# Stacking 64-token halves as even and odd lanes on the way into a 2-D Fourier filter

## The chip, the cores and the metric

One core of a Trainium2 chip runs the whole kernel. The metric is the device time of one execution in microseconds (us); the smaller, the better.

## The reference, cut to what matters

```python
x  = A_x                                  # (1, 2048, 512), bf16
xn = layernorm(x, axis=-1)                # no scale, no bias, eps 1e-5

# A: a global filter in the frequency domain, over tokens and channels
X = rfft2(xn)                             # (2048, 257), complex
y = irfft2(X * (A_w_r + 1j * A_w_i), s=(2048, 512)).astype(bf16)

# B: a gated MLP, 512 -> 1792 -> 512
g, u = xn @ B_w_gate, xn @ B_w_up
return x + y + (gelu_tanh(g) * u) @ B_w_down
```

## The kernel before, in words

**Two bodies of work on five engines.** TensorE (PE) computes the MLP, and matmuls with small cosine and sine matrices for the Fourier part. VectorE (DVE) computes LayerNorm's statistics, the products `gelu(g) * u`, and all sums and differences of the Fourier part. ScalarE (ACT) moves matmul results out of PSUM (L662 applies gelu, L663 copies, L576, L787, L865 and L929 copy results of the Fourier part). GpSimd takes inverse roots, SyncE (SP) issues nearly all DMAs, one after the other, in one queue.

**The order of the work** is written by a planner that runs while the program is built (`_Sched`). Each operation is declared with its engine, an assumed cost and a key. `run` goes through a simulated time: it takes next the operation that could start first, among those of the same engine within 0.05 us the one with the smallest ready time plus key. A PE operation whose inputs come from elsewhere counts as ready 1.0 us late (`MARGIN`, L245). Each engine then runs its list strictly in that order and waits on semaphores. `pool` gives names to small sets of buffers: 3 PSUM banks for `gu` (the MLP's first products), 2 pairs of banks for `sp` (everything of the Fourier part, and the last block's `down`), 1 bank for `dn`, 4 SBUF buffers each for `gg` and `uu`, 28 for `hT`.

**The MLP** is the filler of PE's list. `gated` (L648) makes 8 matmuls for one of 14 column groups of one block of 512 tokens, two evictions on ACT (L662 into `gg`, L663 into `uu`) and one product on DVE (L664 into `hT`, key 1.5). `down` (L692) makes 14 matmuls for 128 tokens, an eviction (L710) and an addition to `x` on DVE (L711); for the last block, DVE adds straight from PSUM (L713).

**The Fourier part** is one long chain, cut into these steps:
1. `stats`, `norm` and `turn` (L503 to L539): LayerNorm of 16 row blocks of 128 tokens, and transposes into `xnT`, 4 row blocks at a time.
2. `fold(b)` (L545), for each group b of 4 row blocks: DVE folds the channels (4 operations), then pairs row blocks, the sum and the difference of one and the mirrored other (L558, L559), into `z`. PE multiplies with the channel transform (L570), 8 matmuls for each of 2 row blocks, and ACT evicts to `Y` (L576).
3. The slot transform (L742 to L764): DVE transforms over 8 slots, for even and odd token parts side by side, from `Y` through `s_`, `v_`, `ab` to `H`, 14 operations.
4. The token matmuls (L767 to L787): for each of 8 groups v of frequencies, the cosine and sine matrices of `tokf` times `H`. Groups 0 and 1 take 2 matmuls, the other six 4: cosine times one part plus sine times the other, for the real and the imaginary result. ACT evicts to `X` (L787).
5. The filter (L794 to L843) on DVE, the way back through tokens (L859, L860) and a 16-slot transform on DVE (L868 to L906), the way back through channels (L924), and the addition to `x` (L937).

`x` is loaded and stored in 16 row blocks; row block s holds tokens of block `(s - 1) % 16` (`blk`, L458). The first four are loaded by one DMA each (L466 to L470), before the weights in SP's queue.

Of the kernel before, what the change touches and what calls it, by code (L numbers as in the profile page):

```python
# [12 lines left out]
S = 2048  # L13
D = 512
FF = 1792
P = 128
# [20 lines left out]
def _constants():  # L37
# [13 lines left out]
    cof[:, 0, 0] *= 0.5  # L51
    tf = np.stack([cof, si2, -si2], 1)
    ci, sv = co[:64].transpose(2, 1, 0), si2[:64].transpose(2, 1, 0)
# [32 lines left out]
class _V:  # L86


    def __init__(self, ap, buf, idx, cell):
        self.ap, self.buf, self.idx, self.cell = ap, buf, idx, cell  # L90

    def __getitem__(self, sl):
        if not isinstance(sl, tuple):
            sl = (sl,)
        return _V(self.ap[sl], self.buf, self.idx[sl[1:]], self.cell)

    def rs(self, shape):
        nd = self.idx.ndim
        ap = self.ap
        names = "abcdef"  # L100
        if nd > 1:
            ap = ap.rearrange("p %s -> p (%s)" % (" ".join(names[:nd]), " ".join(names[:nd])))
        if len(shape) > 1:
            nn = names[:len(shape)]
            ap = ap.rearrange("p (%s) -> p %s" % (" ".join(nn), " ".join(nn)), **dict(zip(nn[1:], shape[1:])))
        return _V(ap, self.buf, self.idx.reshape(shape), self.cell)

    def tr(self, perm):
        names = "abcdef"[:len(perm)]
        ap = self.ap.rearrange("p %s -> p %s" % (" ".join(names), " ".join(names[i] for i in perm)))  # L110
        return _V(ap, self.buf, self.idx.transpose(perm), self.cell)

    def cells(self):
        return [(self.buf, int(c)) for c in np.unique(self.idx // self.cell)]

# [217 lines left out]
def bass_parallel_sum__spectral_gfnet__glu_gated_geglu__prompt_kernel(  # L333
# [14 lines left out]

    xb = A_x[0].rearrange("(a q) d -> q a d", q=P)
    ob = out[0].rearrange("(a q) d -> q a d", q=P)  # L350
    wgv = B_w_gate.rearrange("(dc p) f -> p dc f", p=P)
# [6 lines left out]
    with ExitStack() as es:  # L358
# [22 lines left out]
        small = sb("smallc", [11, P])  # L381
        tf = sb("tokf", [3, 8, P])
        ti = sb("toki", [8, 3, P])
# [73 lines left out]

        def blk(s):  # L458
            return (s - 1) % 16

        def wload(q, dst, src, lo, hi, **kw):
# [79 lines left out]

        Y = R1(0, [8, 2, D])
        H = R3(0, [8, 2, D])
        X = R1(0, [8, 2, D])
        def fold(b):  # L545
            par = b % 2
            a = RB(2048 * par, [4, 2, P])
            f = RB(4096 + 2048 * par, [4, 4, P])
            z = R3(2048 * par, [2, 2, 512])
            xt = xnT[:, b]  # L550
# [4 lines left out]
            tt(f[:, :, 2:4], xt[:, :, 0:2], xt[:, :, 2:4], SUB, 1024, kk)  # L555
            fv = f.rs([2, 2, 4, P])
            zv = z.rs([2, 2, 4, P])
            tt(zv[:, :, 0], fv[:, :, 1], fv[:, :, 0, :, ::-1], ADD, 1024, kk)  # L558
            tt(zv[:, :, 1], fv[:, :, 1], fv[:, :, 0, :, ::-1], SUB, 1024, kk)  # L559
            for j in range(2):  # L560
                t = _T("sp")

                def f_c(e, z=z, j=j, t=t):
                    ins = None
                    for o in range(2):
                        bank = spb(t, o).rearrange("p (s r i) -> p s r i", s=2, r=4)
                        for cc in range(4):
                            to = bank[:, :, 2 * cc] if cc < 2 else bank[:, :, 1::2]
                            mat = Tf.ap[:, cc] if cc < 2 else Tf.ap[:, 2 * cc - 2:2 * cc]
                            ins = e.matmul(to, z.ap[:, j, o, cc * P:(cc + 1) * P], mat, start=(cc == 0), stop=(cc == 3))  # L570
                    return ins

                op("pe", 4 * 0.057 + 4 * 0.11, f_c, reads=(z[:, j], Tf), tiles=(t,), key=kk, lag=0.1)
                jp = 2 * b + j
                yv = Y[:, jp].rs([4, 64, 4])
                op("act", c_act(1024), lambda e, yv=yv, t=t: e.activation(yv.ap, spair(t).rearrange("p (s r i) -> p s i r", s=4, r=4), ACT.Copy),  # L576
                   writes=(yv,), tiles=(t,), key=-0.5)
# [30 lines left out]
        load("sp", wd, wdv, NFC * 131072, key=next(k))  # L608
        load("sp", tf, c_tf.ap().rearrange("p (t v m) -> p t v m", t=3, v=8), 786432, key=next(k))
        load("sp", ti, c_ti.ap().rearrange("p (v t q) -> p v t q", v=8, t=3), 786432, key=next(k))  # L610
# [104 lines left out]
        def store(s0, n, lo=0, w=512):  # L715
            for s in range(s0, s0 + n):
                v = xs(s)[:, lo:lo + w]
                o = op("sp", 0.41, lambda e, s=s, v=v: e.dma_start(ob[:, blk(s), lo:lo + w], v.ap), reads=(v,), dma=256 * w, key=0.0)
                sch.finals.append(o)

# [20 lines left out]

        s_ = RB(0, [4, 1024])  # L742
        v_ = RB(4096, [4, 1024])
        ab = RB(8192, [2, 1024])
        Yf = R1(0, [8, 1024])
        Hf = R3(0, [8, 1024])

        def scale(v, n):
            op("dve", c_ts(n), lambda e: e.tensor_scalar(v.ap, v.ap, float(np.sqrt(0.5)), None, MUL), reads=(v,), writes=(v,))

        tt(s_[:, 0:2], Yf[:, 0:2], Yf[:, 4:6], ADD, 2048)
        tt(v_[:, 0:2], Yf[:, 0:2], Yf[:, 4:6], SUB, 2048)
        tt(s_[:, 2:4], Yf[:, 2:4], Yf[:, 6:8], ADD, 2048)
        tt(v_[:, 2:4], Yf[:, 2:4], Yf[:, 6:8], SUB, 2048)
        tt(ab[:, 0], v_[:, 1], v_[:, 3], SUB, 1024)
        tt(ab[:, 1], v_[:, 1], v_[:, 3], ADD, 1024)
        scale(ab, 2048)
        tt(Hf[:, 4:6], s_[:, 0:2], s_[:, 2:4], SUB, 2048)
        tt(s_[:, 0:2], s_[:, 0:2], s_[:, 2:4], ADD, 2048)
        tt(Hf[:, 0], s_[:, 0], s_[:, 1], ADD, 1024)  # L760
        tt(Hf[:, 1], s_[:, 0], s_[:, 1], SUB, 1024)
        tt(Hf[:, 2:4], v_[:, 0::2], ab, ADD, 2048)
        tt(Hf[:, 6], v_[:, 0], ab[:, 0], SUB, 1024)
        tt(Hf[:, 7], ab[:, 1], v_[:, 2], SUB, 1024)  # L764

        CO, SI, NS = 0, 1, 2
        for v in range(8):  # L767
            c = v // 2
            t = _T("sp")
            if c == 0:  # L770
                seq = ((0, ((CO, H[:, v, 0]),)), (1, ((SI, H[:, v, 1]),)))
                rd = H[:, v]
            else:
                hr, hi = H[:, 2 * c], H[:, 2 * c + 1]
                seq = ((0, ((CO, hr[:, 0]), (NS, hi[:, 1]))), (1, ((CO, hi[:, 0]), (SI, hr[:, 1]))))
                rd = H[:, 2 * c:2 * c + 2]

            def f_t(e, v=v, t=t, seq=seq):
                ins = None
                for r, terms in seq:  # L780
                    for i, (mt, h) in enumerate(terms):
                        ins = e.matmul(spb(t, r), tf.ap[:, mt, v, :], h.ap, start=(i == 0), stop=(i == len(terms) - 1))  # L782
# [91 lines left out]

        def ts(o, a, f, n):
            op("dve", c_ts(n), lambda e: e.tensor_scalar(o.ap, a.ap, float(f), None, MUL), reads=(a,), writes=(o,))

        tt(al[:, 8], U[:, 0], U[:, 1], ADD, 512)
# [31 lines left out]
        for jq in range(4):  # L910
            js = slice(2 * jq, 2 * jq + 2)
            for lo, hi in ((0, 1), (1, 4)) if jq == 0 else ((4 * jq, 4 * jq + 4),):
                a = Yi[:, (lo - 1) % 16:(lo - 1) % 16 + hi - lo]
                tt(zi[:, lo:hi, :, 0:64], a[:, :, 0], a[:, :, 1], ADD, 256 * (hi - lo))
            a = Yi[:, 4 * jq:4 * jq + 4]
            tt(zi[:, 4 * jq:4 * jq + 4, :, 127:63:-1], a[:, :, 0], a[:, :, 1], SUB, 1024)
            for jp in (2 * jq, 2 * jq + 1):
                t = _T("sp")

                def f_b(e, jp=jp, t=t):  # L920
                    ins = None
                    for o in range(2):
                        for cc in range(4):
                            ins = e.matmul(spb(t, o, cc * P, P), zi.ap[:, 2 * jp + o, cc, :], Ti.ap[:, cc, :], start=(cc == 0), stop=(cc == 3))  # L924
                    return ins

                op("pe", 8 * 0.0565, f_b, reads=(zi[:, 2 * jp:2 * jp + 2], Ti), tiles=(t,), lag=0.1)
                rv = R[:, jp].rs([1024])
# [47 lines left out]
```

## Time and profile before

| what | value |
|---|---|
| median of 3 runs | 178.88 us (178.66 to 179.46) |
| the profiled execution, its own time | 178.78 us |
| its span in the profile | 177.0 us |
| PE busy | 172.4 us (97%), 1052 matmuls |
| DVE busy | 137.8 us (78%), 270 instructions |
| ACT busy | 106.4 us (60%), 172 instructions |
| DMA moved | 14.97 MB |

The span runs from the first instruction to the last; 1.78 us of the execution lie around it. Matmuls are pipelined, so one matmul's duration is longer than the time between the starts of two. The chain of work that ended last gives the time that each piece holds up its successor, and the timeline gives start and duration of each instruction.

### The profile page before, as it was taken

Reading aid. Unit: us, or ns where it says so; the run is one execution under the profiler, and the core shown is the slowest. Engines: PE = TensorE matmul, PEld = TensorE weight load, DVE = VectorE, ACT = ScalarE, POOL = GpSimd, SP = SyncE. Lnnn points to the kernel's source line nnn. Section 1 sums busy time; section 2 is a strip of 40 time slices with the busy share of each in tenths; the row PEclk is TensorE's granted clock in tenths of the full one; section 3 lists DMA queues with packets and bytes.
Section 4 is the critical chain, followed back from the end, with each engine's and each line's share of the span. In section 5 each row is a group of like instructions: output and inputs, shape, how many; then the busy total and the mean of one; then the engine's idle time right before and its main releaser. Section 6 shows DMA issues by size and latency. Waiting matters only on the chain.

```text
span 177.0 us, 2757 instructions
## 1 busy us (share of the span) xinstructions
PE 172.4 (97%) x1052; PEld 90.8 (51%) x1052; DVE 137.8 (78%) x270; ACT 106.4 (60%) x172; POOL 10.1 (6%) x19
## 2 busy tenths in 40 slices
PE   7889999999999999999999999999999999999994
PEld 2678665456554444444544644445664444444443
DVE  3869899999969939999999799999599812121931
ACT  3478775658685798363894966363995636362000
POOL 2120420300000230000000000000000000000000
DMA  5999997222363710000000000000004200000311
GB/s 167 335 351 356 349 371 266 61 65 47 66 151 87 176 38 4 0 0 0 0 6 0 0 0 0 0 4 0 0 19 132 91 0 0 0 4 0 119 59 61
DMA packets 17773, 14.97 MB, mean 85 GB/s; under 512 B 1119, under 2 KB 17376, under 8 KB 17760
## 3 DMA queue, kind: packets, MB, share of 16 engines
q1 hardware_dynamic: 16560, 13.94, 26.3%
q10 hardware_dynamic: 1200, 0.85, 1.6%
q8 instruction: 8, 0.13, 0.3%
q14 instruction: 5, 0.04, 0.1%
HBM read 12.70 MB, written 3.15 MB: 90 GB/s over the span
## 4 chain that ended last, share of the span: by engine, by line
PE 93%; DMA 5%; SPq 1%; issue 0%; DVE 0%
PE ps_gu L657 53%; PE ps_dn L702 20%; PE ps_sp L702 7%; PE ps_sp L782 3%; DMA wu<-in_B_w_up_dram 3%; PE ps_sp L570 3%; PE ps_sp L924 2%; PE ps_sp L534 2%; DMA x_sb<-in_A_x_dram 1%; PE ps_sp L859 1%; PE ps_sp L860 1%; SPq L446 1%; DVE x_sb L713 0%
## 5 line engine op out<-in xcount | busy, mean ns | idle before, releaser
L657 PE MATMUL ps_gu<-xnT,wu 128*128 128x512 bf16 (+1 forms) x236 | 56.7, 363 | 0.6 <-DMA wu<-in_B_w_up_dram 0.6
L657 PE MATMUL ps_gu<-xnT,wg 128*128 128x512 bf16 (+1 forms) x236 | 56.7, 363 | 0.0
L663 ACT ACTIVATE uu<-ps_gu 128x512 bf16<-128x512 f32 (+1 forms) x59 | 33.9, 574 | 13.2 <-PE ps_gu L657 12.9
L662 ACT ACTIVATE gg<-ps_gu 128x512 bf16<-128x512 f32 (+1 forms) x59 | 34.0, 576 | 12.2 <-PE ps_gu L657 11.6
L702 PE MATMUL ps_dn<-wd,hT 128*128 128x512 bf16 x168 | 38.5, 379 | 0.0
L657 PEld LDWEIGHTS ps_gu<-xnT,wu 128*128 128x128 bf16 x236 | 22.7, 98 | 22.9 <-ACT uu L688 0.8
L657 PEld LDWEIGHTS ps_gu<-xnT,wg 128*128 128x128 bf16 x236 | 22.6, 98 | 21.5 <-DVE xnT L539 0.3
L664 DVE TENSOR_TENSOR hT<-gg,uu 128x512 bf16<-128x512 bf16 (+1 forms) x59 | 22.7, 394 | 11.6 <-ACT uu L663 11.5
L702 PEld LDWEIGHTS ps_dn<-wd,hT 128*128 128x128 bf16 x168 | 16.4, 98 | 19.4
L450 DVE TENSOR_TENSOR specB<-specB 128x1024 bf16<-128x1024 bf16 (+2 forms) x37 | 23.5, 669 | 2.1 <-ACT specB L929 2.0
L710 ACT ACTIVATE db<-ps_dn 128x512 bf16<-128x512 f32 x12 | 7.2, 597 | 23.4 <-PE ps_dn L702 23.4
L504 DVE BATCH_NORM_STATS2 bst<-x_sb 128x6 f32<-128x512 bf16 x16 | 10.9, 685 | 3.7 <-DMA x_sb<-in_A_x_dram 3.5
L450 DVE TENSOR_TENSOR specB<-specA 128x2048 bf16<-128x2048 bf16 x8 | 9.4, 1220 | 4.0 <-ACT specA L787 2.1
L702 PE MATMUL ps_sp<-wd,hT 128*128 128x512 bf16 (+2 forms) x70 | 12.3, 336 | 0.0
L711 DVE TENSOR_TENSOR x_sb<-db,x_sb 128x512 bf16<-128x512 bf16 x12 | 5.0, 418 | 7.8 <-ACT db L710 7.8
L450 DVE TENSOR_TENSOR specC<-specB 128x1024 bf16<-128x1024 bf16 (+1 forms) x14 | 10.0, 759 | 0.0
L702 PEld LDWEIGHTS ps_sp<-wd,hT 128*128 128x128 bf16 x70 | 6.4, 98 | 6.1 <-DVE x_sb L713 0.2
L450 DVE TENSOR_TENSOR specB<-specB,filt 128x2048 bf16<-128x2048 bf16 x8 | 9.4, 1215 | 0.0
L787 ACT ACTIVATE specA<-ps_sp 128x1024 bf16<-128x1024 f32 x8 | 7.9, 1027 | 2.0 <-PE ps_sp L782 1.9
L929 ACT ACTIVATE specB<-ps_sp 128x1024 bf16<-128x1024 f32 x8 | 8.5, 1090 | 0.0
L576 ACT ACTIVATE specA<-ps_sp 128x1024 bf16<-128x1024 f32 x8 | 7.8, 1021 | 0.3
L865 ACT ACTIVATE specC<-ps_sp 128x1024 bf16<-128x1024 f32 x8 | 7.8, 1042 | 0.0
(63 smaller groups left out, 141.2 us busy)
## 6 DMA issues: line engine op xcount, KB each, us to landing
out_dram<-x_sb SPq DMA_DIRECT2D x15, 128.0 KB, 1.8
wd<-in_B_w_down_dram SPq DMA_DIRECT2D x1, 1792.0 KB, 13.3
x_sb<-in_A_x_dram SPq DMA_DIRECT2D x3, 512.0 KB, 8.4
wg<-in_B_w_gate_dram SPq DMA_DIRECT2D x2, 512.0 KB, 8.4
wu<-in_B_w_up_dram SPq DMA_DIRECT2D x2, 512.0 KB, 8.7
filt<-w_mirror SPq DMA_DIRECT2D x6, 128.5 KB, 2.3
tokf<-c_tf SPq DMA_DIRECT2D x1, 768.0 KB, 13.7
toki<-c_ti SPq DMA_DIRECT2D x1, 768.0 KB, 9.7
```

The costliest lines, as they stand in the source:

```text
L450: return op("dve", c_tt(n), lambda e: e.tensor_tensor(o.ap, a.ap, b.ap, f), reads=(a, b), writes=(o,), key=key, **kw)
L504: op("dve", 0.61, lambda e: e.bn_stats(bst[:, s].ap, xs(s).ap), reads=(xs(s),), writes=(bst[:, s],), key=key, due=due, after=after)
L576: op("act", c_act(1024), lambda e, yv=yv, t=t: e.activation(yv.ap, spair(t).rearrange("p (s r i) -> p s i r", s=4, r=4), ACT.Copy), writes ...
L657: ins = e.matmul(gub(t, n), w.ap[:, dc, fc * P:(fc + 1) * P], xnT.ap[:, b, sl, dc, :], start=(dc == 0), stop=(dc == 3))
L662: op("act", c_act(n), lambda e: e.activation(gg.ap[:, gs.slot, 0:n], gub(g, n), ACT.Gelu_apprx_tanh), tiles=(g, gs), key=0.0)
L663: op("act", c_act(n), lambda e: e.activation(uu.ap[:, us.slot, 0:n], gub(u, n), ACT.Copy), tiles=(u, us), key=0.0)
L664: op("dve", c_tt(n), lambda e: e.tensor_tensor(hT.ap[:, h.slot, lo:lo + n], gg.ap[:, gs.slot, 0:n], uu.ap[:, us.slot, 0:n], MUL), tiles=(g ...
L702: ins = e.matmul(bank(), hT.ap[:, hs[(b, fc)].slot, sl * P:(sl + 1) * P], wd.ap[:, fc, lo:lo + n], start=(fc == 0), stop=(fc == NFC - 1))
L710: op("act", c_act(n), lambda e: e.activation(db.ap[:, d.slot, 0:n], bank(), ACT.Copy), tiles=(t, d), key=0.0)
L787: op("act", c_act(1024), lambda e, xv=xv, t=t: e.activation(xv.ap, spair(t), ACT.Copy), writes=(xv,), tiles=(t,), key=-0.5)
L865: op("act", c_act(1024), lambda e, gv=gv, t=t: e.activation(gv.ap, spair(t).rearrange("p (k x i) -> p k x i", k=4, x=4), ACT.Copy), writes ...
L929: op("act", c_act(1024), lambda e, rv=rv, t=t: e.activation(rv.ap, spair(t), ACT.Copy), writes=(rv,), tiles=(t,), key=-0.5)
```

## The change

The way into the frequency domain is laid out as the way back is already. A row block now holds two 64-token halves around a multiple of 128 (`halves`, with the order `SL`); row block 0 holds the last 64 and the first 64 tokens. `fold` pairs the two halves within a row block instead of two row blocks: the sum goes to lanes 0 to 63 of slot p of `z`, the difference to lanes 64 to 127 of slot p + 4. So a slot of `z` is complete only when the group four slots before it has been folded too: the channel matmuls of group 0 are put off, and group 3 has 4 pairs of slots instead of 2. The slot transform has 16 points instead of 8 and 32 DVE operations instead of 14; six of them work on half of the lanes. Each token matmul contracts over the even and the odd lanes at once, so groups 1 to 7 take 2 matmuls each, and group 0 takes 4: 18 instead of 28. `tokf` shrinks from 768 to 576 KB. The row block of two halves is loaded and stored by two DMAs of 64 rows. On the way back, the operations that fill `zi` change their slices; there are 8 instead of 9.

```diff
+    SL = (1, 2, 3, 0) + tuple(range(4, 16))
-    xb = A_x[0].rearrange("(a q) d -> q a d", q=P)
+    xb = A_x[0][64:S - 64].rearrange("(a q) d -> q a d", q=P)
+    def halves(t, n):
+        return [(slice(0, P), t[0][P * n - 64:P * n + 64])] if n else [(slice(0, 64), t[0][S - 64:S]), (slice(64, P), t[0][0:64])]
...
         for s in range(4):
-            o = load("sp", x[:, s], xb[:, blk(s), :], 131072, key=next(k))
+            for part, rows in halves(A_x, SL[s]):
+                o = load("sp", x[part, s], rows, 1024 * (part.stop - part.start), key=next(k))
...
+        z = R3(0, [16, 4, P])
         def fold(b):
...
-            tt(zv[:, :, 0], fv[:, :, 1], fv[:, :, 0, :, ::-1], ADD, 1024, kk)
-            tt(zv[:, :, 1], fv[:, :, 1], fv[:, :, 0, :, ::-1], SUB, 1024, kk)
-            for j in range(2):
+            for i, n in ((0, 3), (3, 1)) if b == 0 else ((0, 4),):
+                p = SL[4 * b + i]
+                fv = f[:, i:i + n]
+                tt(z[:, p:p + n, :, 0:64], fv[:, :, :, 64:P], fv[:, :, :, 63::-1], ADD, 256 * n, kk)
+                p = (p + 4) % 16
+                tt(z[:, p:p + n, :, 64:P], fv[:, :, :, 64:P], fv[:, :, :, 63::-1], SUB, 256 * n, kk)
+            for p in {0: (), 1: (4, 6), 2: (8, 10), 3: (12, 14, 0, 2)}[b]:
...
+        Fb = RB(0, [24, D])
+        def crossed(o, a, b_, f):
+            tt(o[0:64], a[0:64], b_[0:64], f, 1024)
+            tt(o[64:P, ::-1], a[64:P], b_[64:P], f, 1024)
+        for i in (4, 0):
+            tt(Fb[:, i:i + 4], Y[:, i:i + 4], Y[:, i + 8:i + 12], ADD, 2048)
+            tt(Fb[:, i + 8:i + 12], Y[:, i:i + 4], Y[:, i + 8:i + 12], SUB, 2048)
+        s2, v2 = Fb[:, 16:20], Fb[:, 20:24]
+        tt(s2, Fb[:, 0:4], Fb[:, 4:8], ADD, 2048)
+        tt(v2, Fb[:, 0:4], Fb[:, 4:8], SUB, 2048)
+        crossed(H[:, 12:14], s2[:, 0:2], s2[:, 2:4], SUB)
+        u = Fb[:, 2:4]
+        tt(u, s2[:, 0:2], s2[:, 2:4], ADD, 1024)
+        tt(H[:, 14], u[:, 0], u[:, 1], ADD, 512)
+        tt(H[:, 15], u[:, 0], u[:, 1], SUB, 512)
+        tt(Fb[:, 0], v2[:, 1], v2[:, 3], SUB, 512)
+        tt(Fb[:, 1], v2[:, 1], v2[:, 3], ADD, 512)
+        ts(Fb[:, 0:2], Fb[:, 0:2], C2, 1024)
+        crossed(H[:, 8:10], v2[:, 0::2], Fb[:, 0:2], ADD)
+        crossed(H[:, 10:12], Fb[:, 20:0:-19], Fb[:, 0:23:22], SUB)
+        tt(Fb[:, 2:4], Fb[:, 9:12:2], Fb[:, 15:12:-2], SUB, 1024)
+        tt(Fb[:, 4:6], Fb[:, 9:12:2], Fb[:, 15:12:-2], ADD, 1024)
+        tt(Fb[:, 6], Fb[:, 10], Fb[:, 14], SUB, 512)
+        tt(Fb[:, 7], Fb[:, 10], Fb[:, 14], ADD, 512)
+        ts(Fb[:, 6:8], Fb[:, 6:8], C2, 1024)
+        ts(Fb[:, 16:20], Fb[:, 2:6], C1, 2048)
+        ts(Fb[:, 20:24], Fb[:, 2:6], C3, 2048)
+        tt(Fb[:, 0:2], Fb[:, 8:13:4], Fb[:, 6:8], ADD, 1024)
+        tt(Fb[:, 2:4], Fb[:, 8:13:4], Fb[:, 6:8], SUB, 1024)
+        tt(Fb[:, 4:6], Fb[:, 16:23:6], Fb[:, 21:18:-2], ADD, 1024)
+        tt(Fb[:, 6:8], Fb[:, 20:17:-2], Fb[:, 17:24:6], SUB, 1024)
+        tt(H[:, 0:4], Fb[:, 0:4], Fb[:, 4:8], ADD, 2048)
+        tt(H[:, 4:6], Fb[:, 0:4:2], Fb[:, 4:8:2], SUB, 1024)
+        tt(H[:, 6:8], Fb[:, 5:8:2], Fb[:, 1:4:2], SUB, 1024)
-        for v in range(8):
-            c = v // 2
+        for v, hh in enumerate(((14, 15), (12, 13), (0, 1), (4, 6), (8, 9), (10, 11), (2, 7), (5, 3))):
             t = _T("sp")
...
+                for r in range(2):
+                    if v:
+                        ins = e.matmul(spb(t, r), tf.ap[:, 2 + 2 * v + r], H.ap[:, hh[r]], start=True, stop=True)
+                    else:
+                        for i in range(2):
+                            ins = e.matmul(spb(t, r), tf.ap[:, 2 * r + i], H.ap[:, hh[i]], start=(i == 0), stop=(i == 1))
...
-            op("pe", (2 if c == 0 else 4) * mm(512), f_t, reads=(rd, tf), tiles=(t,), lag=0.1)
+            op("pe", (2 if v else 4) * mm(512), f_t, reads=(H[:, hh[0]], H[:, hh[1]], tf), tiles=(t,), lag=0.1)
```

Not shown are the constants of `tokf`, the bookkeeping that tells the two halves of the lanes apart in the planner's dependencies, the removed slot transform, and the renamed slices of the way back and of `store`.

More of the change, by code (lines that the diff above doesn't have):

```diff
@@ L51, in _constants @@
     cof[:, 0, 0] *= 0.5
-    tf = np.stack([cof, si2, -si2], 1)
+    low = (m < 64)[None]
+    tf = []
+    for a in (cof, si2):
+        for part in (low, ~low):
+            e = a[:64, 0] * part
+            tf.append(np.concatenate([e, 0 * e] if a is cof else [0 * e, e]))
+    for v, c in enumerate((4, 1, 9, 2, 10, 3, 11)):
+        g = -1.0 if c > 8 else 1.0
+        c = min(c, 16 - c)
+        if c % 2:
+            r = np.sin(np.pi * c / 2)
+            f = r * g, r
+        else:
+            f = (-1.0, 1.0) if c == 4 else (g, -1.0)
+        tf.append(np.concatenate([co[:64, v + 1], f[0] * si[:64, v + 1]]))
+        tf.append(np.concatenate([g * co[:64, v + 1], f[1] * si[:64, v + 1]]))
+    tf = np.stack(tf, 1)
     ci, sv = co[:64].transpose(2, 1, 0), si2[:64].transpose(2, 1, 0)
@@ L94, in __getitem__ @@
             sl = (sl,)
-        return _V(self.ap[sl], self.buf, self.idx[sl[1:]], self.cell)
+        lo, hi, _ = sl[0].indices(P)
+        part = tuple(h for h in self.part if lo < 64 * (h + 1) and hi > 64 * h)
+        return _V(self.ap[sl], self.buf, self.idx[sl[1:]], self.cell, part)
     def rs(self, shape):
@@ L569, in f_c @@
                             mat = Tf.ap[:, cc] if cc < 2 else Tf.ap[:, 2 * cc - 2:2 * cc]
[L570 removed]
+                            ins = e.matmul(to, z.ap[:, p + o, cc, :], mat, start=(cc == 0), stop=(cc == 3))
                     return ins
[L573 to L575 removed]
+                op("pe", 4 * 0.057 + 4 * 0.11, f_c, reads=(z[:, p:p + 2], Tf), tiles=(t,), key=kk, lag=0.1)
+                yv = Y[:, p:p + 2].rs([4, 64, 4])
                 op("act", c_act(1024), lambda e, yv=yv, t=t: e.activation(yv.ap, spair(t).rearrange("p (s r i) -> p s i r", s=4, r=4), ACT.Copy),
@@ L608, in bass_parallel_sum__spectral_gfnet__glu_gated_geglu__prompt_kernel @@
         load("sp", wd, wdv, NFC * 131072, key=next(k))
-        load("sp", tf, c_tf.ap().rearrange("p (t v m) -> p t v m", t=3, v=8), 786432, key=next(k))
+        load("sp", tf, c_tf.ap().rearrange("p (t m) -> p t m", t=18), 589824, key=next(k))
         load("sp", ti, c_ti.ap().rearrange("p (v t q) -> p v t q", v=8, t=3), 786432, key=next(k))
@@ L716, in store @@
             for s in range(s0, s0 + n):
-                v = xs(s)[:, lo:lo + w]
-                o = op("sp", 0.41, lambda e, s=s, v=v: e.dma_start(ob[:, blk(s), lo:lo + w], v.ap), reads=(v,), dma=256 * w, key=0.0)
-                sch.finals.append(o)
+                for part, rows in halves(out, SL[s]):
+                    v = xs(s)[part, lo:lo + w]
+                    o = op("sp", 0.41, lambda e, rows=rows, v=v: e.dma_start(rows[:, lo:lo + w], v.ap), reads=(v,), dma=2 * w * (part.stop - part.start), key=0.0)
+                    sch.finals.append(o)
         first(NFIRST)
@@ L739, in bass_parallel_sum__spectral_gfnet__glu_gated_geglu__prompt_kernel @@
                 down(*it[1:])
[L742 to L753, printed above, removed]
```

64 lines of the change are left out of this document (18 added, 46 removed).

## The prediction

> **What bounds the kernel now.** I read the page first, then busy time by stretches, then the chain that ended last.
>
> ```profile
> span 177.0 us, 2757 instructions
> ...
> PE 172.4 (97%) x1052; PEld 90.8 (51%) x1052; DVE 137.8 (78%) x270; ACT 106.4 (60%) x172; POOL 10.1 (6%) x19
> ...
> DVE  3869899999969939999999799999599812121931
> ...
> PE 93%; DMA 5%; SPq 1%; issue 0%; DVE 0%
> ```
>
> PE is busy for 97% of the span and makes up 93% of the chain. DVE is nearly full for three quarters of the span and mostly free in the last quarter. A share of busy time could still hide short waits, so the stretches come next (columns: stretch, its length, then busy us of each engine, clock granted to TensorE, DMA share, GB/s).
>
> ```profile
> 14.00:50.00 36.00, 36.00 (x264) 22.22 (x262) 35.00 (x86) 25.24 (x44) 4.54 (x6) 1.00 0.63 193
> 50.00:137.00 87.00, 87.00 (x502) 43.09 (x501) 79.06 (x133) 60.27 (x90) 2.52 (x2) 1.00 0.11 28
> ```
>
> From 14 to 137 us PE has not one idle moment, at full clock. The chain says the same for its end and shows the channel matmuls of group 0 and the token matmuls (start, length, what):
>
> ```profile
> 21.29 1.32 PE ps_sp L570 x16
> ...
> 57.10 1.73 PE ps_sp L782 x8
> ...
> 61.20 0.86 PE ps_sp L782 x4
> ...
> 162.57 12.14 PE ps_sp L702 x70
> ...
> 174.73 0.29 DVE x_sb L713
> ```
>
> PE runs into the last `down` without a break; behind it come one DVE operation and the last store. So the time is the start, up to PE's first unbroken work, plus the sum of PE's work, plus a short tail. A matmul taken off PE anywhere between is worth its full pitch, as long as PE doesn't begin to wait.
>
> **What the change takes off PE.**
>
> ```profile
> L782 PE MATMUL ps_sp<-specC,tokf 128*128 128x512 bf16 x28 | 6.9, 379 | 0.0
> ```
>
> One matmul lasts 379 ns, but they overlap: the chain has 8 in 1.73 us and 4 in 0.86 us, so each holds PE for 0.216 us. The diff leaves 18 (4 for group 0, 2 for each of seven others): 10 x 0.216 = **2.16 us less**. Channel matmuls, evictions and MLP matmuls keep their number and shapes; group 0's channel matmuls only move. PE's term is -2.16 us.
>
> **What it adds on DVE.** The new slot transform is priced by the start-to-start time of like operations in a row (timeline), with the mean duration of the last one taken off (groups by form).
>
> ```profile
> 69.12 4.63 DVE L450 TENSOR_TENSOR specB<-specB,filt 128x2048 bf16<-128x2048 bf16 x4
> 137.30 1.29 DVE L450 TENSOR_TENSOR specB<-specB 128x1024 bf16<-128x1024 bf16 x2
> 39.32 0.76 DVE L450 TENSOR_TENSOR specB<-specB 128x512 bf16<-128x512 bf16 x2
> 110.55 1.29 DVE L876 TENSOR_SCALAR specB<-specA 128x2048 bf16<-128x2048 bf16 x2
> 112.09 0.42 DVE L876 TENSOR_SCALAR specB<-specB 128x1024 bf16<-128x1024 bf16 x1
> 112.43 0.42 DVE L664 TENSOR_TENSOR hT<-gg,uu 128x512 bf16<-128x512 bf16 x1
> ```
> ```profile
> L450 DVE TENSOR_TENSOR specB<-specB,filt 128x2048 bf16<-128x2048 bf16 x8 | 9.4, 1215 | 0.0
> L450 DVE TENSOR_TENSOR specB<-specB 128x1024 bf16<-128x1024 bf16 x20 | 12.9, 685 | 2.1 <-ACT specB L929 2.0
> L450 DVE TENSOR_TENSOR specB<-specB 128x512 bf16<-128x512 bf16 x12 | 4.6, 416 | 0.0
> L876 DVE TENSOR_SCALAR specB<-specA 128x2048 bf16<-128x2048 bf16 x2 | 1.3, 684 | 0.0
> ```
>
> A sum or difference of 2048 elements takes (4.63 - 1.215) / 3 = 1.14 us, one of 1024 takes 1.29 - 0.685 = 0.60, one of 512 takes 0.76 - 0.416 = 0.34; scaling takes 1.29 - 0.684 = 0.61 for 2048 and 0.34 for 1024 (112.09 to 112.43). Before: 7 of 2048, 6 of 1024 and one scaling of 2048, 7.98 + 3.60 + 0.61 = 12.2 us. After: 7 of 2048, 15 of 1024 (six on 64 lanes, counted like full ones), 6 of 512, and scalings of 1024 and 2048, two each: 7.98 + 9.00 + 2.04 + 0.68 + 1.22 = 20.9 us. That is **8.7 us more DVE work**, and it lies on the Fourier chain. Two smaller pieces in `fold` (group 0 in 4 operations instead of 2) and one operation less on the way back nearly cancel.
>
> **What covers it.** The chain's end has room:
>
> ```profile
> 138.84 1.29 DVE L450 TENSOR_TENSOR specB<-specB 128x1024 bf16<-128x1024 bf16 x2
> ...
> 163.23 0.43 DVE L711 TENSOR_TENSOR x_sb<-db,x_sb 128x512 bf16<-128x512 bf16 x1 [2.60 <-ACT db L710]
> 163.69 1.23 DVE L450 TENSOR_TENSOR x_sb<-specB,x_sb 128x2048 bf16<-128x2048 bf16 x1
> ```
>
> By 140.1 us the chain has done what it can; its last additions to `x` wait until 163.23 for the MLP's L711, which PE sets. With PE 2.16 us earlier that is 161.1, so the cover is 21 us. Against it stand 8.7 us, stretched to about 10.8 because gate products run between (0.34 us in every 1.73, PE's 8 matmuls of 0.216 for one column group); two more evictions behind group 3's folding; and two evictions more at the end, because the last three operations now release four groups of frequencies at once and the filter's first half needs two of them.
>
> ```profile
> 49.78 1.94 ACT L576 ACTIVATE specA<-ps_sp 128x1024 bf16<-128x1024 f32 x2
> ```
>
> Two of these evictions take 1.94 us, so the two extra behind folding cost about 1.9 us of delay, and the two behind the transform as much. In all (10.8 + 1.9 + 1.9) some 15 us of the 21 (an estimate from these rows): the chain still ends about 6 us early. DVE does not reach the end; if that cover were gone, each further us of delay would cost one.
>
> **What moves.** Group 0's 16 channel matmuls (1.32 us of PE at 21.29) go behind group 3's folding. What PE does instead is the MLP of block 0.
>
> ```profile
> 18.54 1.03 PE L657 MATMUL ps_gu<-xnT,wg 128*128 128x512 bf16 x4
> ...
> 26.61 0.68 DVE L539 COPY xnT<-ps_sp 128x1024 bf16<-128x1024 bf16 x1
> ```
>
> At 18.54 begin the last 8 column groups of block 0, 1.73 us each, so even without channel matmuls and transposes they last to 32.4 us; block 1 is transposed by 27.3. That leaves 5.1 us, so PE does not run dry: cost 0, at most 1.3. Group 3 then sends four evictions through ACT's queue; the MLP's evictions L662 and L663 stand behind them, and PE's `gu` banks behind those. But with two `sp` pairs the third and fourth can't start before the first two are evicted, so MLP work comes between: cost 0.
>
> **The start.** The load of row block 3 becomes two DMAs, one more issue ahead of everything that follows in SP's queue.
>
> ```profile
> 4.13 0.43 SPq L446 DMA_DIRECT2D wg<-in_B_w_gate_dram  x1
> 4.60 0.51 SPq L446 DMA_DIRECT2D wu<-in_B_w_up_dram  x1
> ...
> 10.49 0.60 PE L657 MATMUL ps_gu<-xnT,wu 128*128 128x256 bf16 x4 [0.56 <-DMA wu<-in_B_w_up_dram]
> ```
> ```profile
> 4.00:6.00 2.00, 1.90 (x8) 0.53 (x6) 1.46 (x6) 1.74 (x3) 0.68 (x2) 1.00 1.09 353
> 10.00:12.00 2.00, 1.51 (x18) 1.44 (x19) 1.26 (x5) 1.58 (x5) 0.00 (x0) 1.00 1.10 351
> ```
>
> An issue takes 0.47 us (4.13 to 4.60), and PE waits 0.56 us for this very `wu`, so the upper bound is 0.47. But the DMA engines are full (share 1.09 and 1.10) from 4 to 12 us: bytes set the landing more than issues do, and the bytes are the same. The lower bound is -0.5, if planning anew hid that wait. I take +0.2, nearer to the row of the full engines.
>
> **The sum.** Against the profiled execution's own 178.78 us: 178.78 - 2.16 + 0.2 = 176.8. The median of the runs lies 0.1 above that execution, so the forecast is 176.9 us.
>
> **The rivals.** *Late handovers, 178.9 us.* PE's list is fixed when the program is built, and DVE's new forms could be slower than planned; PE would then stand at a token matmul whose `H` is late.
>
> ```profile
> 59.12 3.63 DVE L450 TENSOR_TENSOR specC<-specB 128x1024 bf16<-128x1024 bf16 x5
> ...
> 61.03 1.03 PE L782 MATMUL ps_sp<-specC,tokf 128*128 128x512 bf16 x4
> ```
> ```profile
> L713 DVE TENSOR_TENSOR x_sb<-ps_sp,x_sb 128x512 bf16<-128x512 f32 x3 | 2.1, 691 | 2.8 <-PE ps_sp L702 2.7
> L713 DVE TENSOR_TENSOR x_sb<-ps_sp,x_sb 128x128 bf16<-128x128 f32 x1 | 0.3, 292 | 0.2 <-PE ps_sp L702 0.2
> ```
>
> The first result of that group is there at 59.12 + 0.685 = 59.8 at the earliest, PE takes it at 61.03: the slack is at most 1.2 us. The slowest form of an addition in the trace is L713, (691 - 292) / 384 = 1.04 ns per element; at that rate 1024 elements take 1.22 us instead of 0.685, and the six half-lane operations 3.2 us more. Minus the slack of 1.2, PE would stand 2.0 us: no change. Against it: no operation from SBUF to SBUF in the trace of before runs at that rate, mirrored ones included. None of them starts at lane 64, so I can't exclude it.
>
> By the Trainium skill, "VectorE: DVE Perf Modes", section "What auto-detection actually checks", a two-input operation runs at double rate if every tensor has 16 bits and step 1 or -1; the new operations keep that within a row, so by the page this rival falls away. The same page, section "Two Vector instructions with no wait between them", says that an instruction starting in another quarter of the lanes than the one before is held until all earlier ones have finished; by it each of six switches would lose the overlap of 0.685 - 0.60, together some 0.5 us, less than the slack. No row of before shows a switch to lane 64.
>
> *Starved gate products, 182.3 us, slower.* The new transform is 20.9 us of DVE work, and the planner lets an old ready operation pass a gate product (key 1.5). Without gate products ACT can't refill `gg`, `gu` fills up, and PE stops.
>
> ```profile
> 98.72 0.74 DVE L664 TENSOR_TENSOR hT<-gg,uu 128x512 bf16<-128x512 bf16 x2
> ...
> 108.88 0.42 DVE L664 TENSOR_TENSOR hT<-gg,uu 128x512 bf16<-128x512 bf16 x1
> ```
>
> Before, the 16-slot transform of the way back kept gate products out for 10 us and PE did not wait. PE has 4 `gg` buffers (4 x 1.73 = 6.9 us), 3 banks (2.6 us) and about two `down` (14 x 0.216 = 3.02 us each): 15.5 us. A gap of the full 20.9 would stop PE for 5.4 us: 176.9 + 5.4 = 182.3. From a gap of 17.5 us on the kernel would be slower than before. Against it: the new transform is mostly one chain, where the next operation becomes ready only when the last has ended, so waiting gate products get in.
>
> *PE runs dry early, 178.2 us.* If block 1's transposes came so late that block 0's MLP work ended first, PE would miss the channel matmuls moved away and stand for their 1.3 us: 176.9 + 1.3. The 5.1 us above speak against it.
>
> **How the numbers follow.** A measurement of this kernel can tell 0.5%, 0.9 us. The forecast has 0.68, with its own range of 176.2 to 177.6 (start from -0.5 to +0.47, and small waits). Late handovers have 0.12 and running dry 0.05, both within 0.5% of before. Starved gate products have 0.15, slower. So faster 0.68, same 0.17, slower 0.15. The range from 176.2 to 179.6 takes in all but the starved case.
>
> **What would show it.** Right: 18 matmuls from `tokf`, PE still without idle time from 14 us to the last `down`, DVE busy near 146.6 us, and the last `down` beginning near 160.6. The half-lane operations should show about 0.685 us. Wrong: idle time of PE ahead of a token matmul (late handovers), ACT's L662 or L663 waiting for DVE and PE for ACT between 50 and 90 us (starved), a longer wait for `wu` at 10 us (start), or the last additions L937 later than L711 at the end (cover gone).

## The result, and the profile after

The changed kernel takes 176.94 us (median of 4 runs, 176.70 to 177.05) against 178.95 us: the ratio is 0.988, with an interval from 0.986 to 0.991. So it is 1.2% faster, 2.0 us; the forecast was 176.9 us. The profiled execution has a span of 175.3 us, 1.7 us less than before (177.0).

The page of the changed kernel (the same rows as shown of before):

```profile
span 175.3 us, 2759 instructions
...
PE 170.2 (97%) x1042; PEld 89.8 (51%) x1042; DVE 146.4 (84%) x289; ACT 106.2 (61%) x172; POOL 11.3 (6%) x19
...
DVE  3769999999819999976999999969999939982931
...
PE 92%; DMA 4%; SPq 1%; issue 0%; DVE 0%
```

PE has 10 matmuls less and 2.2 us less busy time; DVE has 8.6 us more, and its full stretch now reaches further into the last quarter. PE is still the chain. Busy time by stretches (same columns as before):

```profile
14.00:50.00 36.00, 36.00 (x255) 21.67 (x253) 33.30 (x87) 23.95 (x44) 4.17 (x6) 1.00 0.66 196
50.00:137.00 87.00, 87.00 (x477) 42.48 (x475) 80.50 (x137) 58.83 (x91) 3.96 (x2) 1.00 0.09 21
```

PE is without idle time from 14 to 137 us, as before. The chain that ended last (start, length, what), its beginning and its end:

```profile
5.50 5.35 DMA wu<-in_B_w_up_dram
10.85 0.14 issue
10.98 1.03 PE ps_gu L679 x8
...
13.78 9.73 PE ps_gu L679 x68
...
62.57 0.43 PE ps_sp L813 x2
...
160.86 12.14 PE ps_sp L724 x70
173.00 0.02 issue
173.02 0.29 DVE x_sb L735
```

The lines have moved: L679 is L657 of before, L813 and L816 are the token matmuls, L724 is `down`, L735 is L713. A group of frequencies with two matmuls holds PE for 0.43 us, where one with four held it for 0.86. From the first `wu` matmul after the wait to PE's end are 173.00 - 10.98 = 162.02 us, against 174.70 - 10.49 = 164.21 before: 2.19 us less. The beginning is 0.49 us later. That is the whole difference of the spans.

DVE's new operations on half of the lanes, and what follows them (timeline):

```profile
66.28 0.68 DVE L472 TENSOR_TENSOR specB<-specB 128x1024 bf16<-128x1024 bf16 x1
66.89 2.83 DVE L472 TENSOR_TENSOR specC<-specB 64x1024 bf16<-64x1024 bf16 x4
69.75 0.69 DVE L768 TENSOR_SCALAR specB<-specB 128x2048 bf16<-128x2048 bf16 x1
```
```profile
L472 DVE TENSOR_TENSOR specC<-specB 64x1024 bf16<-64x1024 bf16 x6 | 4.1, 683 | 0.1
```

One takes 683 ns, like a full-lane operation. Four in a row start every (2.83 - 0.683) / 3 = 0.72 us instead of every 0.60.

The end of the Fourier chain (timeline of DVE):

```profile
154.51 1.28 DVE L472 TENSOR_TENSOR specB<-specB 128x1024 bf16<-128x1024 bf16 x2
...
161.53 0.43 DVE L733 TENSOR_TENSOR x_sb<-db,x_sb 128x512 bf16<-128x512 bf16 x1 [2.60 <-ACT db L732]
161.99 1.22 DVE L472 TENSOR_TENSOR x_sb<-specB,x_sb 128x2048 bf16<-128x2048 bf16 x1
```

The chain has done what it can at 155.8 us instead of 140.1, and its next addition still waits behind the MLP's L733 until 162.0: 6.2 us of cover are left, where before it waited 23.6 us (140.1 to 163.69).

### The profile page after: what moved, and what is told of

It is laid out like the page before. It is cut to its first block, busy times and chain, and to the rows that moved or that the text cites. A ratio compares the mean times of both kernels' runs of the same rounds, so it can differ in the third digit from the quotient of the medians.

```text
span 175.3 us, 2759 instructions
## 1 busy us (share of the span) xinstructions
PE 170.2 (97%) x1042; PEld 89.8 (51%) x1042; DVE 146.4 (84%) x289; ACT 106.2 (61%) x172; POOL 11.3 (6%) x19
## 4 chain that ended last, share of the span: by engine, by line
PE 92%; DMA 4%; SPq 1%; issue 0%; DVE 0%
PE ps_gu L679 54%; PE ps_dn L724 21%; PE ps_sp L724 7%; DMA wu<-in_B_w_up_dram 3%; PE ps_sp L593 3%; PE ps_sp L953 2%; PE ps_sp L554 2%; PE ps_sp L813 2%; DMA x_sb<-in_A_x_dram 1%; SPq L468 1%; PE ps_sp L893 1%; PE ps_sp L894 1%; PE ps_sp L816 0%; DVE x_sb L735 0%
## 5 line engine op out<-in xcount | busy, mean ns | idle before, releaser
L679 PE MATMUL ps_gu<-xnT,wu 128*128 128x512 bf16 (+1 forms) x236 | 56.7, 363 | 0.7 <-DMA wu<-in_B_w_up_dram 0.7
L679 PE MATMUL ps_gu<-xnT,wg 128*128 128x512 bf16 (+1 forms) x236 | 56.7, 363 | 0.0
L724 PE MATMUL ps_dn<-wd,hT 128*128 128x512 bf16 x168 | 38.9, 379 | 0.0
L679 PEld LDWEIGHTS ps_gu<-xnT,wu 128*128 128x128 bf16 x236 | 22.7, 98 | 22.9 <-ACT gg L684 0.9
L679 PEld LDWEIGHTS ps_gu<-xnT,wg 128*128 128x128 bf16 x236 | 22.6, 98 | 21.8 <-DVE xnT L559 0.3
L472 DVE TENSOR_TENSOR specB<-specB 128x1024 bf16<-128x1024 bf16 (+2 forms) x47 | 29.2, 659 | 1.5 <-ACT specB L958 1.4
L724 PEld LDWEIGHTS ps_dn<-wd,hT 128*128 128x128 bf16 x168 | 16.4, 98 | 19.6
L472 DVE TENSOR_TENSOR specC<-specB 128x1024 bf16<-128x1024 bf16 (+5 forms) x21 | 12.5, 628 | 0.1
L724 PE MATMUL ps_sp<-wd,hT 128*128 128x512 bf16 (+2 forms) x70 | 12.3, 336 | 0.0
L724 PEld LDWEIGHTS ps_sp<-wd,hT 128*128 128x128 bf16 x70 | 6.3, 98 | 6.1 <-DVE x_sb L735 0.2
L733 DVE TENSOR_TENSOR x_sb<-db,x_sb 128x512 bf16<-128x512 bf16 x12 | 5.0, 415 | 4.4 <-ACT db L732 4.4
L958 ACT ACTIVATE specB<-ps_sp 128x1024 bf16<-128x1024 f32 x8 | 7.8, 1031 | 0.8 <-PE ps_sp L953 0.8
```

What stands on the lines that cost most here:

```text
L472: return op("dve", c_tt(n), lambda e: e.tensor_tensor(o.ap, a.ap, b.ap, f), reads=(a, b), writes=(o,), key=key, **kw)
L679: ins = e.matmul(gub(t, n), w.ap[:, dc, fc * P:(fc + 1) * P], xnT.ap[:, b, sl, dc, :], start=(dc == 0), stop=(dc == 3))
L724: ins = e.matmul(bank(), hT.ap[:, hs[(b, fc)].slot, sl * P:(sl + 1) * P], wd.ap[:, fc, lo:lo + n], start=(fc == 0), stop=(fc == NFC - 1))
L958: op("act", c_act(1024), lambda e, rv=rv, t=t: e.activation(rv.ap, spair(t), ACT.Copy), writes=(rv,), tiles=(t,), key=-0.5)
```

## The experiments

**The two parts alone.** First the split load alone, in the kernel before (the bookkeeping that tells the two halves of the lanes apart goes with it and isn't shown):

```diff
-            o = load("sp", x[:, s], xb[:, blk(s), :], 131072, key=next(k))
+            for lo, hi in ((0, 64), (64, P)) if s == 3 else ((0, P),):
+                o = load("sp", x[lo:hi, s], xb[lo:hi, blk(s), :], 1024 * (hi - lo), key=next(k))
```

> The kernel before, with one part of the change alone: the load of row block 3 is split into two DMAs of 64 rows on SP's queue. Theory (issues pace the start): the changed kernel began its unbroken PE work 0.49 us later (13.78 against 13.29 us) because one more DMA issue stands ahead of the weights; then this kernel is 0.5 us slower than before, about 179.4 us, with wu landing near 10.85 instead of 10.35 us. Rival (bytes pace the start, as the prediction weighed it): same bytes, same landing, 178.9 us, and the changed kernel's later start comes from somewhere else in the change.

Measured: 179.12 us, ratio 1.0015 (0.999 to 1.0041). The issues behave as expected, PE's start does not (timeline of this kernel):

```profile
3.37 1.57 SPq L448 DMA_DIRECT2D x_sb<-in_A_x_dram  x3
4.98 0.59 SPq L448 DMA_DIRECT2D wg<-in_B_w_gate_dram  x1
5.61 0.51 SPq L448 DMA_DIRECT2D wu<-in_B_w_up_dram  x1
...
10.23 0.60 PE L660 MATMUL ps_gu<-xnT,wu 128*128 128x256 bf16 x4 [0.22 <-DMA wu<-in_B_w_up_dram]
```

`wu` is issued 1.0 us later than before (5.61 against 4.60) and is there at least as early: PE's wait for it ends at 10.23 us instead of 10.49. So a later issue by itself doesn't fix the landing. The interval of the time, 0.2 us less to 0.7 us more, neither excludes nor shows 0.5 us.

Then ten matmuls less, and nothing else:

```diff
                 for r, terms in seq:
+                    terms = terms[:1] if 2 <= v < 7 else terms
```

> The kernel before, with 10 of its 28 token matmuls left out (the second terms of five of the six groups that have four; the output lacks them) and nothing else changed: DVE's work, the slot transform and the loads stay. Theory (PE's sum sets the time): 10 x 0.216 = 2.16 us less, about 176.8 us, span 174.8 us, PE still without a gap. Rival (the Fourier chain or DVE sets part of the time): less than 1 us gained, and PE shows idle time where the matmuls were.

Measured: 177.69 us, ratio 0.992 (0.990 to 0.995): 1.25 us by the medians (0.9 to 1.8 by the interval), not 2.16. PE got waits that neither the kernel before nor the changed one has (timeline of PE):

```profile
42.10 1.50 PE L570 MATMUL ps_sp<-smallc,specC 128*128 128x128 bf16 x16 [0.47 <-DVE xnT L539]
64.84 0.60 PE L783 MATMUL ps_sp<-specC,tokf 128*128 128x512 bf16 x2 [0.42 <-ACT specA L788]
```

The first lies ahead of the edit and comes from row blocks 8 to 11, which landed later in this execution (DVE could begin on them at 21.58 us instead of 20.54). The second is the edit's own: with half the matmuls per group, PE offers results faster than ACT evicts them, and the slot transform of before delivers them in one go. In this profile PE's stretch from the first `wu` matmul to its end is 163.40 us (10.43 to 173.83), only 0.81 less than the 164.21 of before. The rows show 0.89 us of waiting, of which the second, 0.42, is a matter of the order of work; how much of the 0.9 us that the medians miss is due to it, no run separates. In the changed kernel the slot transform is longer, its groups come spread from 62 to 79 us, and no such wait is in its profile.

The changed kernel again, beside them:

> The changed kernel again, on the same chip as the parts. Expected 176.9 us as on record; the two parts alone (the split load, and ten matmuls fewer) should add up to it: +0.5 and -2.16, so -1.7 against before.

Measured: 176.89 us, ratio 0.989 (0.986 to 0.993). PE's work from the first `wu` matmul to its end is again 162.0 us (11.13 to 173.16). The parts as measured don't add up to it (+0.2 and -1.25 against -2.05); the ten matmuls are worth more in the changed kernel than alone in the one before.

**The price of a matmul in the changed kernel.** Ten matmuls are put back, without use (the planner's cost for these groups is raised with them, not shown):

```diff
                     if v:
-                        ins = e.matmul(spb(t, r), tf.ap[:, 2 + 2 * v + r], H.ap[:, hh[r]], start=True, stop=True)
+                        for _ in range(2 if v < 6 else 1):
+                            ins = e.matmul(spb(t, r), tf.ap[:, 2 + 2 * v + r], H.ap[:, hh[r]], start=True, stop=True)
```

> The changed kernel, with the matmuls of five groups issued twice (10 matmuls more, each overwriting its own result; same output). Theory (PE's sum sets the time, a matmul is worth its pitch): +2.16 us, about 179.1 us. Rival (what ten fewer matmuls showed in the kernel before, 1.25 us, is their real worth because PE waits elsewhere): +1.25 us, about 178.1 us.

Measured: 178.88 us, ratio 0.998 (0.996 to 1.001) to the kernel before. That is 2.0 us more than the changed kernel's 176.89, measured on another chip, and 1.6 to 1.8 us more by the ratios to before; the times alone don't decide between 2.16 and 1.25. On the same chip the changed kernel with a moved load, below, takes 176.75 and 176.67 us, 2.1 to 2.2 less. Its chain and its first `wu` matmul:

```profile
10.71 0.60 PE L679 MATMUL ps_gu<-xnT,wu 128*128 128x256 bf16 x4 [0.53 <-DMA wu<-in_B_w_up_dram]
```
```profile
171.40 3.45 PE ps_sp L724 x29
174.85 0.02 issue
```

From 10.71 to 174.85 are 164.14 us, 2.12 us more than 162.02. So in this profile each matmul is worth its pitch, 0.212 us, and the gain of PE's stretch goes when ten of them return.

**The start.** Three kernels move the load of row block 3, or a part of it, to ACT's queue, for the kernel before (there in one piece) and for the changed one (shown here):

```diff
+                if s == 3:                       # e3_half_on_act: s == 3 and part.start
+                    load("act", x[part, s], rows, 65536, key=0.6)
+                    continue
```

> The kernel before, with the load of row block 3 issued from ACT's queue behind ACT's two weight loads instead of from SP's: one issue less ahead of SP's weights. Theory (issues pace the start): wu lands up to 0.47 us earlier, PE's wait of 0.56 us shrinks, about 178.4 to 178.6 us. Rival (bytes pace the start): 178.9 us, and wu lands at 10.3 us as before.

Measured: 178.66 us, ratio 0.999 (0.997 to 1.002): nothing that can be told from before. PE waits for no `wu` any more, but 0.29 us for a transposed row block instead.

> The changed kernel, with the second of the two half-row-block loads issued from ACT's queue (behind its two weight loads, ahead of its first activation) instead of SP's. Theory (the split starves the DMA engines): in all profiles with two half loads on SP, wg and wu were issued 0.7 to 0.9 us later than before and the DMA engines moved only 191 to 206 GB/s from 6 to 8 us against 324; with one issue off SP that gap shrinks and PE's unbroken work begins near 13.3 instead of 13.8 us, about 176.4 us. Rival (the start moves by itself from run to run, since the split alone left PE's start at 13.26 us): no change, 176.9 us.

Measured: 176.75 us, ratio to before 0.986 (0.983 to 0.988), which takes in the 0.988 of the changed kernel. From 6 to 8 us the DMA engines move 260 GB/s instead of the changed kernel's 201, so the gap did shrink, but PE's unbroken work begins at 13.74 us, as in the changed kernel (13.78).

> The changed kernel, with both half loads on ACT's queue, so that SP issues its weights even earlier than in the kernel before. Theory (issues feed the DMA engines): no gap from 6 to 8 us, wu lands at 10.3 us or earlier, PE's unbroken work begins near 13.3 us or earlier, 176.2 to 176.5 us. Rival (the start moves by itself): 176.9 us. A third way: ACT issues for 1.2 us more, and its first activation at 4.2 us is late or row block 3 lands later than before; then 177 us or more.

Measured: 176.67 us, ratio to before 0.987 (0.983 to 0.990). The wait for `wu` is gone, but the medians of the three kernels lie within 0.3 us. In this profile the first matmuls took 0.63 us for four instead of 0.39 until 10.4 us, so its start can't be compared. Whether one of these loads belongs on ACT's queue stays open; nothing here is worth 0.5 us.

A further profile of before was to tell how much the start moves by itself:

> The kernel before, one more profile. Profiles of kernels with the loads of before began their unbroken PE work (the first wu matmul after the wait) at 10.49, 10.43 and 10.34 us, those with the split load on SP at 10.98, 11.13, 10.71 and 10.23 us. Expected 10.3 to 10.5 us here, and from there to the end of PE's last matmul 164.2 us, against 162.0 us in both profiles of the changed kernel. A second thing to see is the first matmul L570 of group 1 near 41.5 us: PE waited there for DVE's copy L539 in two of four profiles of this order of work.

Measured: 178.98 us; the first `wu` matmul starts at 10.71 us and PE ends at 174.92: 164.2 us, as expected. The start is later than expected, behind a wait for ACT instead of `wu`, and PE did not wait near 41.5 us. (Of the three starts that the expectation names for the loads of before, 10.34 belongs to the kernel with row block 3 on ACT's queue.) Over ten profiles (all in which SP issues these loads, but for that of the starved gate products below), the matmul with which PE's unbroken work begins (13.29 us in the profile of before) starts at 13.29, 13.23, 13.42 and 13.51 us where row block 3 is one load, and at 13.78, 13.94, 13.49, 13.58, 13.56 and 13.26 us where it is two on SP: 13.36 and 13.60 on average, 0.24 us apart, with the two sets overlapping.

One more theory on the kernel before came from this. PE stood at 41.8 and 42.1 us for DVE in the two parts alone, behind row blocks 8 to 11. So these were loaded earlier in the kernel before (they are taken out of their old place, not shown):

```diff
         for lo, hi in ((768, 1280), (1280, FF)):
+            if lo == 1280:
+                load("sp", x[:, 8:12], xb[:, 7:11, :], 524288, key=next(k))
```

> The kernel before, with the load of row blocks 8 to 11 moved ahead of the last columns of the gate and up weights in SP's queue. In profiles of this kernel with small edits, PE waited 0.2 to 0.5 us near 41.8 us for DVE's copy L539, behind a chain that starts with these row blocks landing at 20.5 to 21.6 us. Theory (the kernel before stands on that edge, which adds to its time and its spread): with an earlier landing the wait can't arise, 178.4 to 178.7 us and a narrower spread than 178.1 to 180.6 us. Rival: the weights land later in exchange or the planner moves the wait elsewhere; 178.9 us or more.

Measured: 178.91 us, ratio 1.0002 (0.998 to 1.0025). The wait at 41.8 us is not in the profile, and nothing is gained; the spread, 178.1 to 180.2 us, isn't narrower than that of before in the same series, 178.5 to 179.9. The theory falls as an account of the time of before, whose two profiles don't have that wait either.

**The cover.** Multiplications by 1.0 lengthen the chain inside the slot transform:

```diff
+        for _ in range(6):                       # e6_chain_18_more: 18
+            ts(Fb[:, 0:4], Fb[:, 0:4], 1.0, 2048)
         tt(H[:, 0:4], Fb[:, 0:4], Fb[:, 4:8], ADD, 2048)
```

> The changed kernel, with 6 multiplications by 1.0 (2048 elements each, one after the other, same output) put into the slot transform ahead of its last three operations: about 4.1 us more on the Fourier chain. In the profile of the changed kernel the chain's last free work ends at 155.8 us and its last additions wait for L733 of the MLP at 161.96, so 6.2 us are left. Theory (PE sets the time while the chain fits under it): no change, 176.9 us. Rival (DVE nearly full already costs PE time): each further us shows, 179 us or more.

Measured: 176.72 us, ratio to before 0.989 (0.987 to 0.991): no change against the changed kernel, though DVE is busy for 3.5 us more (149.9 against 146.4). The chain's last free work (timeline of DVE):

```profile
159.22 1.29 DVE L472 TENSOR_TENSOR specB<-specB 128x1024 bf16<-128x1024 bf16 x2
```

It ends at 160.5 instead of 155.8 us: 4.7 us of the cover are used, and PE's end does not move.

> The changed kernel, with 18 such multiplications by 1.0 instead of 6: about 12.4 us more DVE work, stretched by gate products to some 15 us of delay, 9 us over the 6.2 us of cover. Theory: the chain now ends last and PE waits for it near the end: about 186 us, with idle PE ahead of the last channel matmuls or the last down. If the time stays at 176.9 us, the cover was larger than read from the profile.

Measured: 186.77 us, ratio to before 1.045 (1.041 to 1.048). From 14 us on, PE has its one long wait at the end (timeline of PE, and busy time by stretches, columns as before):

```profile
160.41 6.21 PE L724 MATMUL ps_sp<-wd,hT 128*128 128x512 bf16 x27
174.25 9.15 PE L724 MATMUL ps_sp<-wd,hT 128*128 128x512 bf16 x42 [7.63 <-DVE x_sb L735]
```
```profile
174.00:180.00 6.00, 5.75 (x14) 2.10 (x15) 0.79 (x2) 0.00 (x0) 0.00 (x0) 0.50 0.13 44
```

The last block's `down` has two pairs of banks. Their additions L735 stand behind the chain's last ones on DVE, so the third `down` can't start. So the chain sticks out by 7.6 us, not by the 9 expected. The time rose by 9.8 us all the same, because PE was slower after the wait: the clock granted to it was 0.50 from 174 to 180 us, and the last 42 matmuls took 9.15 us, where in the changed kernel they take 12.14 - 28 x 0.216 = 6.1. That the time came so near to the forecast of 186 is luck in part: a shorter wait and a slower clock behind it. The cover itself holds: 4.7 us fit under 6.2, and with the longer chain PE waits.

**Starved gate products.** The rival that would have made the kernel slower, forced:

```diff
-HKEY = 1.5
+HKEY = 20.0
```

> The changed kernel, with the key of gate products and block additions on DVE raised from 1.5 to 20 us in the planner, so that every ready operation of the Fourier part passes them; DVE's list then has a stretch of some 16 filter operations of 2048 elements, about 18 us, without one gate product. Rival of the prediction (starved gate products): PE's buffers last 15.5 us, so PE stops for some 3 us there and ACT's gelu waits for DVE: about 180 us. If PE finds other work all the same, 177 us, and the rival's buffer count was wrong.

Measured: four runs from 223.68 to 227.11 us, ratio to before 1.254 (1.249 to 1.260), far more than the 180 us expected. DVE's gate products around the filter (timeline of DVE), PE's next MLP matmul (timeline of PE) and the busy time of two stretches:

```profile
75.94 0.43 DVE L686 TENSOR_TENSOR hT<-gg,uu 128x512 bf16<-128x512 bf16 x1 [2.96 <-ACT uu L685]
...
99.28 0.41 DVE L686 TENSOR_TENSOR hT<-gg,uu 128x512 bf16<-128x512 bf16 x1
```
```profile
100.37 1.04 PE L679 MATMUL ps_gu<-xnT,wu 128*128 128x512 bf16 x4 [2.72 <-ACT gg L684]
```
```profile
14.00:50.00 36.00, 22.83 (x174) 16.18 (x175) 30.40 (x79) 13.29 (x26) 4.83 (x6) 0.76 0.66 197
...
76.00:99.00 23.00, 18.31 (x105) 8.72 (x105) 21.10 (x29) 11.73 (x17) 0.00 (x0) 1.00 0.00 0
```

In the 23 us without a gate product PE had about 15 us of MLP work, four column groups and two and a half `down`: the buffer count of the prediction (15.5) was about right. It was idle for 4.7 us, not for 23 - 15.5 = 7.5, because its list also had token matmuls there, which the count leaves out. Of these 4.7 us some 3.3 are waits for other evictions and for results of the filter. The wait for ACT's gelu, which the starved case is about, begins at 97.7 us and lasts 2.72 us; over the whole span there are four of them, 11.9 us together.

The edit did more harm where it wasn't aimed: from 14 to 50 us LayerNorm and folding passed the gate products too, PE was busy for 22.8 of 36 us, and its granted clock fell to 0.76. Over the span PE's idle time grew from 5.1 to 36.1 us, and the same matmuls kept it busy for 185.8 us instead of 170.2, at a mean granted clock of 0.91. So this run doesn't price a single gap cleanly. The mechanism is real, then, and it costs far more than the 5.4 us of the prediction when it strikes in several places. What the changed kernel shows is that it doesn't strike: there the longest gap lies between the three gate products that begin at 76.71 us and the one at 87.63, and PE has no idle time from 14 to 137 us.

## Why the prediction was right

**PE's term** (-2.16 us by the pitch) measured -2.19 us in the profile as recorded, and +2.12 when ten matmuls came back. That PE's sum sets the time of the changed kernel is shown by the last, by its row of the profile more than by the medians; ten fewer in the kernel before gave only 1.25 us, because there PE began to wait. The prediction had named that condition ("as long as PE doesn't begin to wait").

**DVE's term** (+8.7 us): busy time went from 137.8 to 146.4 us, +8.6. The half-lane operations took 683 ns, as forecast, but they start every 0.72 us and not every 0.60, as the price had it.

**The cover** (some 15 of 21 us used up, 6 left): the chain's end moved by 15.7 us, and 6.2 us were left (5.7 if counted to the start of L733, as the 21 were counted). The total was right, its parts only in part. The last eviction of folding, the end of the slot transform and the first operation of the filter show them, the first row of before, the others of after (timelines of DVE and ACT):

```profile
66.66 2.36 DVE L450 TENSOR_TENSOR specB<-specA 128x2048 bf16<-128x2048 bf16 x2 [2.05 <-ACT specA L787]
```
```profile
53.60 1.10 ACT L598 ACTIVATE specA<-ps_sp 128x1024 bf16<-128x1024 f32 x1
74.37 2.42 DVE L472 TENSOR_TENSOR specC<-specB 128x2048 bf16<-128x2048 bf16 x3
80.28 2.36 DVE L472 TENSOR_TENSOR specB<-specA 128x2048 bf16<-128x2048 bf16 x2 [2.49 <-ACT specA L821]
```

With the rows of before that the prediction shows (49.78 and 59.12), the last eviction ends at 54.7 us instead of 51.7, 3.0 later where 1.9 were forecast. From there the transform ends after 22.1 us instead of 11.0, 11.1 more where 10.8 were forecast. From its end to the filter pass 3.5 us instead of 3.9, where 1.9 more were forecast. Behind that the chain lost another 2.0 us, which the prediction doesn't have. That these errors cancel is luck.

**The start** (+0.2 us) is the weakest step. The profile showed +0.49, just past the upper bound of 0.47, and one of its reasons was wrong: the DMA engines did not stay full. Busy time by stretches, columns as before:

```profile
6.00:8.00 2.00, 1.58 (x29) 1.59 (x30) 1.86 (x6) 0.04 (x1) 0.19 (x1) 1.00 1.08 324
```
```profile
6.00:8.00 2.00, 1.63 (x27) 1.48 (x28) 1.45 (x4) 0.00 (x1) 0.15 (x1) 1.00 0.84 201
```

The first row is of before, the second of after: 324 GB/s became 201. The issues of after (SP's queue):

```profile
4.87 0.59 SPq L468 DMA_DIRECT2D wg<-in_B_w_gate_dram  x1
5.50 0.52 SPq L468 DMA_DIRECT2D wu<-in_B_w_up_dram  x1
```

`wg` came 0.74 us later than before (4.87 against 4.13) and `wu` 0.90 us (5.50 against 4.60), not 0.47. Over ten profiles the difference of the starts is 0.24 us, near the forecast, but with a scatter as large as itself; that the split costs 0.2 us is therefore plausible, not shown.

**The sum** (176.9 us) met the measured 176.94 more closely than its terms are known: the start scatters by 0.3 us, and the median of before lay between 178.92 and 179.18 us in its four series. The agreement to 0.04 us is luck; that the gain is near 2 us is not.

**Late handovers** did not come. By the Trainium skill, "VectorE: DVE Perf Modes", section "What auto-detection actually checks", the double rate was to be kept, and the trace agrees (683 ns). The hold on a change of lanes (same page, section "Two Vector instructions with no wait between them") fits the trace too: 0.72 instead of 0.60 us per start, 0.12 us where I had worked out 0.08, and no PE time. The argument from the trace of before was too wide: sums and products of 512 elements or more keep below 1.04 ns per element there (416 ns for 512), but BATCH_NORM_STATS2, from SBUF to SBUF, takes 685 ns for 512 elements. **Starved gate products** needed a gap of 17.5 us; the longest was about 10, no longer than in the kernel before. **Running dry early** did not come either: PE has no gap at 14 to 50 us.

## What to carry to other kernels

When one engine works without a break, price an edit by the start-to-start time of what it takes off that engine, and spend the rest of the effort on whether the engine will begin to wait: ten matmuls were worth about 1.25 us (0.9 to 1.8) in one kernel, where PE began to wait, and 2.1 in another, where it didn't. Work added to an engine that looks nearly full can be free; the number to look for is the last wait of the chain it lies on, and how long that wait is, here 23.6 us before and 6.2 after. Once the engine does wait, the loss can be more than the wait: behind 7.6 us of waiting PE had a granted clock of 0.50 and lost some 3 us more. A difference of half a microsecond in the start of one profile is no finding yet: here a second profile of the changed kernel had it too (13.94 us), and four others with the split load began at 13.26 to 13.58.

## What was not expected of the hardware

In the changed kernel each of the two 64-row loads held SP's queue for about 0.63 us, from issue to issue, where the same load in one piece had held it for 0.48 (from 3.65 to 4.13 us in the profile of before). It isn't only their shape: `wg` behind them is the same load in both kernels and held the queue for 0.63 us (4.87 to 5.50) instead of 0.47 (4.13 to 4.60). What makes an issue longer there is not known. Weights issued 1.0 us later landed no later in one kernel, and weights issued 0.9 us later landed 0.5 us later in another with the same loads up to there. Operations on 64 lanes that alternate between lanes 0 and 64 start 0.12 us further apart than full ones of the same size. After 7.6 us without work PE's granted clock was 0.50 for some 6 us.
